# Layer 2 two inner blocks behind layer 1 in a fused attention and MLP kernel, with a third buffer for the inner activations

## The chip, the cores and the metric

The kernel runs on one core of a Trainium2 chip. TensorE (PE) multiplies, VectorE (DVE), ScalarE (ACT) and GpSimd (POOL) work on elements, and SyncE's queue (SP) issues the transfers. Each engine takes its instructions strictly in the order in which the program lists them, and waits at the head of its list for semaphores of the others. The metric is the time of one execution in microseconds (us); smaller is better.

## What is computed

Attention with two kinds of masks gives x, a mixing over the tokens of low rank is added to it, and a two-layer MLP stands behind:

```python
scores = scale * np.matmul(q, k.transpose(0, 1, 3, 2))        # B=8, H=8, S=576, D=64
scores = np.where(masks[None, :, :, :], scores, -1000000000.0)  # a window of 32 keys, plain or dilated by 4
attn = softmax(scores); x = np.matmul(attn, v)                 # x: 8 x 576 x 512
h = xt @ U @ V                                                 # rank 32, over the tokens
u = x + h.transpose(0, 2, 1)
ch = np.maximum(u @ w_ch1, 0.0) @ w_ch2                        # 512 -> 2048 -> 512
return (u + ch).astype(np.float32)
```

## The kernel before, in words

The 4608 tokens are 36 tiles of 128. The MLP takes them in twelve **chunks** of three tiles (384 tokens). The 2048 inner features are sixteen **inner blocks** of 128 (`f` from 0 to 15). All products that must be exact to float32 are split into a high and a low part (names ending in h and l), and three of the four products of parts are taken.

For each chunk the loop at L761 goes over the sixteen inner blocks. `layer1(f)` (L732) issues twelve matmuls (L738) into one PSUM tile `ph`: four with the high weights and high input `uth`, four with the low weights, four with the low input `utl`. ACT then makes the high half of the rectified result, `hh` (L743), and DVE the low half, `hl`, from `ph` and `hh` (L744). `layer2(f)` (L748) issues nine matmuls (L755) from `hh` and `hl` into the chunk's three accumulators `acc`. Before the change the loop issues layer 1 of block f and then layer 2 of block f-1. At the chunk's end DVE adds the accumulators to x (L780), and SP sends the tiles out (L781).

Three sets of buffers close this circle. `ph` has two buffers in PSUM, so `layer1(f+2)` can't start before ACT and DVE have read `ph` of block f. `hh` and `hl` have two each in SBUF (L741, L742). The three accumulators have one buffer each, so the next chunk's first layer 2 waits for L780.

Between the matmuls the loop calls `slot()`, which pops due work from a sorted queue (L726): attention of the next batches (scores `s` L376 and L387, masks and maxima on DVE L404 and L407, exponentials on ACT L411, transposes of the probabilities `pt` on DVE L437 and L440, products `pv` L448, their scaling L476), the mixing over tokens (`xhl` L494 and L496, `t` L516, `ts` L525 to L531, `m` L540, sum L542), and the transposes `xt` of x for the next chunks (L556), sixteen small DVE instructions for each tile. ACT and DVE turn these into `uth` and `utl` (L571, L572). In the first chunk the loop also calls `weight_step` (L262), which narrows the weights from eight-byte numbers on ACT, DVE and POOL (L202 to L220).

The program text doesn't fix the order on an engine. A scheduler goes over the instructions with a timeline of its own, and lists on each engine the ready instruction with the highest priority, which is its place in the program text. So a change to the text also moves work of the attention, on all engines.

## Time and profile before

| what | value |
|---|---|
| median of three runs | 1083.85 us (1081.57 to 1084.34) |
| span of the profiled execution, first to last instruction | 1079.6 us |
| time of the profiled execution outside its span | not listed apart; the lowest of the runs is 2.0 us above the span, the median 4.25 us |
| granted TensorE clock, mean | 0.968 |
| PE busy | 1006.9 us, 93% of the span |
| DVE busy | 793.5 us, 73% |
| ACT busy | 407.4 us, 38% |
| POOL busy | 337.7 us, 31% |
| chain that ended last | PE 62%, DVE 28%, DMA 4%, rest 6% |

A row of the timeline gives the start, the duration, the engine, the source line, the operation with output and input, the number of instructions that it merges, and in brackets how long the engine had been idle and what ended that. A row of the stretches gives, for a stretch of the span, its length, then the busy time and the number of instructions of PE, of its weight loads (PEld), of DVE, ACT and POOL, the granted clock of TensorE, and the share and rate of the DMA engines. The page merges twelve or nine matmuls of one block where nothing stands between them. A matmul's own duration is longer than its distance to the next one, since they are pipelined; the distances are what adds up.

### The profile page before, as it was taken

How to read it: one execution, taken by the hardware profiler on the slowest of the kernel's cores; microseconds unless marked ns; L12 is line 12 of the kernel's file. 1: busy time of each engine (PE TensorE's matmuls, PEld its weight loads, DVE VectorE, ACT ScalarE, POOL GpSimd, SP SyncE). 2: the span in 40 equal slices, each digit the busy share in tenths (PEclk: the TensorE clock that was granted, in tenths of full speed). 3: DMA queues.
4: the chain of work that ended last, by engine and by line, in shares of the span. 5: the costliest groups of instructions: out<-in, count | busy, mean ns of one | idle time of the engine just before them, and what ended most of it. 6: DMA issues, size and time to landing. Idle time of an engine off the chain costs nothing.

```text
span 1079.6 us, 17590 instructions
## 1 busy us (share of the span) xinstructions
PE 1006.9 (93%) x5304; PEld 896.3 (83%) x5304; DVE 793.5 (73%) x2688; ACT 407.4 (38%) x1225; POOL 337.7 (31%) x533
## 2 busy tenths in 40 slices
PE   6688888999999999998999999998999999699998
PEld 6468776988888988987888898897888998599997
DVE  6999998788589778787668878888858876921211
ACT  5566645434234533433323442543324542111110
POOL 1567766243132521242312441433214331000000
PEclk9679999999999999998999999998999999999999
DMA  9556633222222420331202430332302320000000
GB/s 290 165 195 206 208 108 108 72 79 64 65 58 69 122 66 22 102 90 50 79 23 61 114 93 23 103 87 57 92 9 71 101 76 16 30 1 1 30 1 30
DMA packets 75599, 87.33 MB, mean 81 GB/s; under 512 B 10448, under 2 KB 66320, under 8 KB 75504
## 3 DMA queue, kind: packets, MB, share of 16 engines
q1 hardware_dynamic: 75504, 86.20, 26.8%
q8 instruction: 43, 0.70, 0.3%
q14 instruction: 52, 0.43, 0.1%
HBM read 72.00 MB, written 9.44 MB: 75 GB/s over the span
## 4 chain that ended last, share of the span: by engine, by line
PE 62%; DVE 28%; DMA 4%; issue 3%; ACT 1%; POOL 1%; SPq 0%; DVEq 0%; ACTq 0%; POOLq 0%
PE ph L738 28%; PE acc L755 27%; DVE xt L556 9%; PE pv L448 3%; DVE v L211 2%; PE s L376 2%; DVE hl L744 2%; DVE pt L437 2%; DVE pt L440 1%; DVE v L207 1%; PE t L516 1%; DVE p L407 1%; DVE x L476 1%; DVE x L542 1%; DVE xp L476 1%
## 5 line engine op out<-in xcount | busy, mean ns | idle before, releaser
L755 PE MATMUL acc<-w2h,hh 128*128 128x512 f32 x576 | 229.7, 399 | 6.8 <-ACT hh L743 4.5
L352 POOL TENSOR_TENSOR qks<-qkr,qks 128x160 fp32r<-128x160 f32 x192 | 103.8, 540 | 414.5 <-ACT qks L351 259.1
L755 PE MATMUL acc<-w2h,hl 128*128 128x512 f32 x576 | 208.3, 403 | 23.6 <-DVE hl L744 23.4
L755 PE MATMUL acc<-w2l,hh 128*128 128x512 f32 x576 | 228.0, 396 | 0.0
L744 DVE SCALAR_TENSOR_TENSOR hl<-ph,hh 128x384 fp32r<-128x384 f32 x192 | 106.1, 554 | 145.7 <-ACT hh L743 144.5
L411 ACT ACTIVATE p<-p,nmax 128x160 f32<-128x160 f32 (+1 forms) x288 | 116.8, 406 | 202.1 <-DVE nmax L407 200.2
L743 ACT ACTIVATE hh<-ph 128x384 fp32r<-128x384 f32 x192 | 93.2, 485 | 237.5 <-PE ph L738 233.3
L738 PE MATMUL ph<-uth,w1l 128*128 128x384 f32 x768 | 177.6, 343 | 0.0
L738 PE MATMUL ph<-uth,w1h 128*128 128x384 f32 x768 | 176.9, 346 | 0.2 <-ACT uth L571 0.2
L738 PE MATMUL ph<-utl,w1h 128*128 128x384 f32 x768 | 175.8, 341 | 0.1
L738 PEld LDWEIGHTS ph<-uth,w1h 128*128 128x128 f32 x768 | 141.9, 193 | 16.0 <-ACT uth L571 0.6
L556 DVE STREAM_TRANSPOSE xt<-x 32x128 f32<-32x128 f32 x480 | 145.2, 302 | 11.9 <-PE t L516 4.6
L755 PEld LDWEIGHTS acc<-w2h,hl 128*128 128x128 f32 x576 | 107.1, 191 | 51.7 <-DVE hl L744 32.0
L738 PEld LDWEIGHTS ph<-uth,w1l 128*128 128x128 f32 x768 | 138.4, 191 | 0.9
L738 PEld LDWEIGHTS ph<-utl,w1h 128*128 128x128 f32 x768 | 137.0, 189 | 1.5 <-DVE utl L572 0.5
L437 DVE STREAM_TRANSPOSE pt<-p 32x128 f32<-32x128 f32 x384 | 115.7, 301 | 18.6 <-ACT p L411 13.4
L755 PEld LDWEIGHTS acc<-w2h,hh 128*128 128x128 f32 x576 | 108.9, 189 | 23.9 <-ACT hh L743 5.3
L755 PEld LDWEIGHTS acc<-w2l,hh 128*128 128x128 f32 x576 | 108.8, 189 | 15.3
L351 ACT CAST qks<-qkr 128x288 fp32r<-128x288 f32 x192 | 80.9, 428 | 99.2 <-PE s L376 61.2
L355 POOL TENSOR_TENSOR qks<-qkr,qks 64x128 fp32r<-64x128 f32 x192 | 89.6, 467 | 15.1
L448 PE MATMUL pv<-v,pt 96*128 96x128 f32 x576 | 81.5, 286 | 9.5 <-issue 2.9
L448 PEld LDWEIGHTS pv<-v,pt 96*128 96x128 f32 x576 | 77.4, 200 | 14.4 <-issue 6.0
(68 smaller groups left out, 1098.4 us busy)
## 6 DMA issues: line engine op xcount, KB each, us to landing
qkr<-qk SPq DMA_DIRECT2D x192, 144.0 KB, 2.1
raw<-w SPq DMA_DIRECT2D x26, 512.0 KB, 4.4
v<-vv SPq DMA_DIRECT2D x126, 96.0 KB, 2.1
out<-x SPq DMA_DIRECT2D x36, 256.0 KB, 2.3
qkr<-qk SPq DMA_DIRECT2D x22, 224.0 KB, 4.3
qk<-qk SPq DMA_DIRECT2D x7, 448.0 KB, 7.2
raw<-w SPq DMA_DIRECT2D x12, 256.0 KB, 3.2
x<-xp SPq DMA_DIRECT2D x88, 32.0 KB, 1.9
```

Source lines behind the costliest of these rows:

```text
L211: nc.vector.scalar_tensor_tensor(out=o, in0=hi, scalar=-0x80000000, in1=o, op0=ALU.bitwise_and, op1=ALU.bitwise_or)
L351: nc.scalar.copy(out=t[:, 0:QK2], in_=raw)
L352: nc.gpsimd.tensor_tensor(out=t[:, QK2:], in0=raw[:, P:], in1=t[:, P:QK2].bitcast(F32), op=ALU.subtract)
L355: eng.tensor_tensor(out=t[lo, 0:P], in0=raw[lo, 0:P], in1=t[lo, 0:P].bitcast(F32), op=ALU.subtract)
L411: nc.scalar.activation(out=p_sb[:, u, 0:w], in_=p_sb[:, u, 0:w], func=AF.Exp, bias=nmax[:, u:u + 1], scale=-1.0, accum_out=ssum[:, u:u + 1],)
L437: nc.vector.transpose(out=to[:, :, WIN * (r % 2):WIN * (r % 2 + 1)], in_=p_sb[rs, :, QB * s + WIN * k:QB * s + WIN * (k + 1)])
L448: nc.tensor.matmul(pv[:, u, :], lhsT=pt[:, u, :], rhs=v_sb[:, u % 2, :], start=True, stop=True)
L556: nc.vector.transpose(out=tp[ks, :, rs], in_=x4[rs, :, ks])
L738: nc.tensor.matmul(ph, lhsT=w[:, k, :], rhs=u[:, k, :], start=(n == 0), stop=(n == len(seq) - 1))
L743: nc.scalar.activation(out=hh, in_=ph, func=AF.Relu)
L744: nc.vector.scalar_tensor_tensor(out=hl, in0=ph, scalar=0.0, in1=hh.bitcast(F32), op0=ALU.max, op1=ALU.subtract)
L755: nc.tensor.matmul(acc[i], lhsT=h[:, ss], rhs=w, start=(f == 0 and n == 0), stop=(f == FC - 1 and n == 2))
```

## The change

Layer 2 of block f-2, and no longer of f-1, follows layer 1 of block f. `hh` and `hl` get three buffers. At a chunk's end the last two blocks of layer 2 follow the loop. The room for the buffers comes from a scratch area in SBUF for dynamic DMA, which shrinks to 1024 bytes a partition. `ph` keeps its two buffers and `acc` its one each.

```diff
+LAG2 = 2
...
+SCRATCH = 1024
...
-            hh = work.tile([P, CTOK], F32R, tag="hh", name=f"hh{c}_{f}", bufs=2)
-            hl = work.tile([P, CTOK], F32R, tag="hl", name=f"hl{c}_{f}", bufs=2)
+            hh = work.tile([P, CTOK], F32R, tag="hh", name=f"hh{c}_{f}", bufs=LAG2 + 1)
+            hl = work.tile([P, CTOK], F32R, tag="hl", name=f"hl{c}_{f}", bufs=LAG2 + 1)
...
-            if f > 0:
-                layer2(f - 1)
+            if f >= LAG2:
+                layer2(f - LAG2)
                 if f < FC - 1:
                     slot()
...
-        layer2(FC - 1)
+        for f in range(FC - LAG2, FC):
+            layer2(f)
...
-    nc = bacc.Bacc("TRN2", target_bir_lowering=False, num_devices=1)
+    nc = bacc.Bacc("TRN2", target_bir_lowering=False, num_devices=1, dynamic_dma_scratch_size=SCRATCH)
```

The two added constants move the later lines: what is L738 before is L740 after, L744 is L746, L755 is L757, L556 is L558. Names below end in the block (for `ph`, `hh`, `hl`) or the tile (for `acc`) and a running number.

**TensorE, fifth chunk, around inner blocks 10 to 13.** Before, PE comes to the low half of block 10 behind six matmuls of its own block, and to `ph` of block 12 behind that:

```order
L755 MATMUL acc_2_4941<-w2h_762,hh_10_5722 128x512
L755 MATMUL acc_2_4941<-w2l_763,hh_10_5722 128x512
L376 MATMUL s_3_5549<-qks_5513 128x320
L448 MATMUL pv_5593<-v_0_5465,pt_75 128x128 x2
L448 MATMUL pv_5593<-v_1_5483,pt_75 128x128 x2
L755 MATMUL acc_0_4939<-w2h_762,hl_10_5723 128x512
L755 MATMUL acc_1_4940<-w2h_762,hl_10_5723 128x512
L755 MATMUL acc_2_4941<-w2h_762,hl_10_5723 128x512
L738 MATMUL ph_12_5876<-uth_4877,w1h_760 128x384 x4
```

Now the same `s` and `pv` of the attention stand behind six matmuls of block 11, and then comes layer 1 of block 13, ahead of the low half of block 11:

```order
L757 MATMUL acc_2_4933<-w2h_762,hh_11_5770 128x512
L757 MATMUL acc_2_4933<-w2l_763,hh_11_5770 128x512
L378 MATMUL s_3_5551<-qks_5518 128x320
L450 MATMUL pv_5598<-v_0_5468,pt_75 128x128 x2
L450 MATMUL pv_5598<-v_1_5486,pt_75 128x128 x2
L740 MATMUL ph_13_5919<-uth_4843,w1h_1384 128x384 x4
L740 MATMUL ph_13_5919<-uth_4843,w1l_1385 128x384 x4
L740 MATMUL ph_13_5919<-utl_4844,w1h_1384 128x384 x4
L757 MATMUL acc_0_4931<-w2h_762,hl_11_5771 128x512
```

`ph_13` takes the buffer of `ph_11`, so the first of these rows that needs `hl_11` to be done is now the one of `ph_13`, a whole block of layer 1 ahead of the matmul that reads `hl_11`.

**VectorE at the same place.** The transposes `xt` of two tiles are due here. Before, they stand between `hl_9` and `hl_10`; these are the last rows of that stretch:

```order
L556 STREAM_TRANSPOSE xt_5643<-x_3813 32x4x32 x3
L407 ISA p_5497,nmax_5498<-s_1_5511,p_5497 128x160
L407 ISA nmax_5498 128x1
L556 STREAM_TRANSPOSE xt_5643<-x_3813 32x4x32 x6
L404 TENSOR_TENSOR p_5497<-s_2_5535,wide_sb 128x160
L556 STREAM_TRANSPOSE xt_5643<-x_3813 32x4x32
L744 SCALAR_TENSOR_TENSOR hl_10_5723<-ph_10_5686,hh_10_5722 128x384
L556 STREAM_TRANSPOSE xt_5643<-x_3813 32x4x32 x4
L744 SCALAR_TENSOR_TENSOR hl_11_5819<-ph_11_5776,hh_11_5818 128x384
```

Now they stand between `hl_10` and `hl_11`, and `hl_11` behind the last of them:

```order
L558 STREAM_TRANSPOSE xt_5645<-x_3815 32x4x32 x8
L409 ISA p_5502,nmax_5503<-s_1_5516,p_5502 128x160
L409 ISA nmax_5503 128x1
L452 RECIPROCAL ssum_5389<-ssum_5389 128x4
L558 STREAM_TRANSPOSE xt_5645<-x_3815 32x4x32 x2
L406 TENSOR_TENSOR p_5502<-s_2_5535,wide_sb 128x160
L558 STREAM_TRANSPOSE xt_5645<-x_3815 32x4x32 x6
L746 SCALAR_TENSOR_TENSOR hl_11_5771<-ph_11_5731,hh_11_5770 128x384
L746 SCALAR_TENSOR_TENSOR hl_12_5881<-ph_12_5849,hh_12_5880 128x384
```

Counted over the whole stretch, from one `hl` to the next, there are 36 transposes, three L404 and two L407 before, and 40 transposes, four of what was L404 and three of what was L407 now; the other rows are the same. The eighth chunk has 36 and 40 at the same place. In the second chunk the same transposes were spread before, 26 ahead of `hl_9` and 13 ahead of `hl_10`; now 40 stand in one piece ahead of `hl_11`.

**TensorE, end of the first chunk.** Here the mixing of the second batch (`t_1`, then `m_0_1` to `m_4_1`) must be done before the second chunk's first tiles can be turned (`tp`). Before, the last `t_1` stands ahead of eight matmuls of layer 1, and the `m` are strewn into layer 2 of block 15:

```order
L516 MATMUL t_1_1615<-xhl_4_1_1648,us 64x256
L738 MATMUL ph_15_1889<-uth_641,w1l_1404 128x384 x4
L738 MATMUL ph_15_1889<-utl_642,w1h_1403 128x384 x4
L540 MATMUL m_0_1_1675<-ts_1_1667,vs 128x256
L540 MATMUL m_1_1_1687<-ts_1_1667,vs 128x256
L540 MATMUL m_2_1_1698<-ts_1_1667,vs 128x256
L755 MATMUL acc_0_764<-w2h_1405,hh_15_1927 128x512
```

Now layers 1 and 2 of block 15 are over when the last seven `t_1` come, and `m` and `tp` follow with no matmul of the MLP between them:

```order
L757 MATMUL acc_2_766<-w2h_1386,hl_15_1894 128x512
L518 MATMUL t_1_1617<-xhl_1_1_1620,us 64x256
L518 MATMUL t_1_1617<-xhl_2_1_1629,us 64x256 x2
L518 MATMUL t_1_1617<-xhl_3_1_1642,us 64x256 x2
L518 MATMUL t_1_1617<-xhl_4_1_1653,us 64x256 x2
L542 MATMUL m_0_1_1683<-ts_1_1670,vs 128x256
L542 MATMUL m_1_1_1692<-ts_1_1670,vs 128x256
L542 MATMUL m_2_1_1698<-ts_1_1670,vs 128x256
L542 MATMUL m_3_1_1710<-ts_1_1670,vs 128x256
L542 MATMUL m_4_1_1721<-ts_1_1670,vs 128x256
L571 MATMUL tp_1899<-id_sb,x_305 128x128 x4
```

So eight matmuls of layer 1 and nine of layer 2 that lay between the last `t_1` and the first `tp` now lie ahead of it.

**VectorE at that place.** Before, the last `xhl`, which the last `t_1` need, comes straight ahead of `ts_1`, and the three sums of the accumulators only later:

```order
L496 TENSOR_TENSOR xhl_4_1_1648<-x_1039,xhl_4_1_1648 128x256
L526 TENSOR_TENSOR ts_1_1667<-t_1_1615,ts_1_1667 32x256
L542 TENSOR_TENSOR x_344<-x_344,m_0_1_1675 64x256
L744 SCALAR_TENSOR_TENSOR hl_15_1928<-ph_15_1889,hh_15_1927 128x384
L542 TENSOR_TENSOR x_890<-x_890,m_1_1_1687 128x256
```

Now all three stand ahead of `ts_1`, and two of them ahead of the last `xhl`:

```order
L783 TENSOR_TENSOR x_178<-acc_0_764,x_178 128x512
L783 TENSOR_TENSOR x_219<-acc_1_765,x_219 128x512
L498 TENSOR_TENSOR xhl_4_1_1653<-x_1087,xhl_4_1_1653 128x256
L783 TENSOR_TENSOR x_261<-acc_2_766,x_261 128x512
L528 TENSOR_TENSOR ts_1_1670<-t_1_1617,ts_1_1670 32x256
L544 TENSOR_TENSOR x_344<-x_344,m_0_1_1683 64x256
```

`hl_15`, which stood behind the first sum of `m`, now stands ahead of all of these.

## The prediction

> **What bounds the kernel now.** I read the page first: PE is busy for 93% of the span, and no other engine comes near.
>
> ```profile
> span 1079.6 us, 17590 instructions
> PE 1006.9 (93%) x5304; PEld 896.3 (83%) x5304; DVE 793.5 (73%) x2688; ACT 407.4 (38%) x1225; POOL 337.7 (31%) x533
> ```
>
> The 72.7 us in which PE is idle are not spread evenly, so next I took the stretches (length, then PE, PEld, DVE, ACT, POOL busy, clock, DMA):
>
> ```profile
> 40.00:80.00 40.00, 29.90 (x123) 23.94 (x123) 37.97 (x83) 21.94 (x56) 26.70 (x22) 0.63 0.49 162
> 80.00:120.00 40.00, 34.86 (x199) 31.73 (x199) 39.15 (x93) 25.23 (x64) 31.11 (x24) 0.96 0.64 203
> 120.00:160.00 40.00, 33.64 (x193) 28.93 (x193) 38.42 (x128) 21.19 (x70) 25.94 (x25) 1.00 0.45 140
> ...
> 200.00:920.00 720.00, 699.86 (x3748) 627.92 (x3747) 565.63 (x2033) 274.20 (x844) 220.68 (x414) 0.99 0.24 69
> 920.00:948.00 28.00, 19.45 (x81) 15.94 (x80) 26.80 (x80) 3.26 (x7) 0.00 (x0) 0.85 0.08 29
> ```
>
> From 40 to 160 us, the start and most of the first chunk, DVE is busy for 115.5 of 120 us: it sets the pace there, and a longer lead of PE gives nothing but DVE's own 4.5 idle us. From 200 to 920 us PE is idle for 720 - 699.9 = 20.1 us only, and from 920 to 948 us for 8.6 us, again under a full DVE. These 28.7 us are all that a better order can win behind the first chunk, besides what a lowered clock costs. The waits of PE say what they are:
>
> ```profile
> PE acc L755 <- DVE hl L744: 23.4, 20, 2.5
> ...
> PE acc L755 <- ACT hh L743: 4.5, 3, 3.3
> ...
> 105.01 0.50 PE L755 MATMUL acc<-w2h,hh 128*128 128x512 f32 x1 [3.28 <-ACT hh L743]
> ```
>
> (The last row is from the timeline.) Twenty waits of layer 2 for the low half, 23.4 us, none over 2.5 us. This is what the change aims at. The timeline shows where the longest sit. In the fifth chunk:
>
> ```profile
> 474.04 1.05 PE L448 MATMUL pv<-v,pt 96*128 96x128 f32 x8
> ...
> 474.80 0.56 DVE L744 SCALAR_TENSOR_TENSOR hl<-ph,hh 128x384 fp32r<-128x384 f32 x1 [0.83 <-ACT hh L743]
> ...
> 479.26 2.19 DVE L556 STREAM_TRANSPOSE xt<-x 32x128 f32<-32x128 f32 x7
> ...
> 481.48 0.33 DVE L404 TENSOR_TENSOR p<-s,wide_sb 128x160 f32<-128x160 f32 x1
> ...
> 485.90 0.33 DVE L407 CUSTOM_DVE_ANT_0 p<-s,p 128x160 f32<-128x160 f32 x1
> ...
> 486.38 0.38 PE L376 MATMUL s<-qks 128*128 128x320 f32 x1 [2.51 <-DVE nmax L407]
> ...
> 487.66 1.13 PE L448 MATMUL pv<-v,pt 96*128 96x128 f32 x8 [0.90 <-DVE nmax L407]
> ...
> 490.20 0.56 DVE L744 SCALAR_TENSOR_TENSOR hl<-ph,hh 128x384 fp32r<-128x384 f32 x1
> ...
> 490.81 1.65 PE L755 MATMUL acc<-w2h,hl 128*128 128x512 f32 x3 [2.02 <-DVE hl L744]
> ```
>
> DVE does `hl` of block 9 at 474.80 and that of block 10 at 490.20. The 15.4 us between are full of transposes for the next chunk. PE runs out of work and waits three times, 2.51 + 0.90 + 2.02 = 5.4 us. The same burst returns at 735 us. The one in the second chunk is milder, with one wait of 2.09 us:
>
> ```profile
> 735.00:739.00 4.00, 1.51 (x6) 0.75 (x5) 3.80 (x14) 0.90 (x3) 0.00 (x0) 0.91 0.23 69
> 739.00:742.00 3.00, 2.31 (x9) 2.05 (x10) 2.80 (x11) 0.84 (x3) 0.97 (x2) 0.50 0.09 22
> ...
> 237.70 0.98 PE L755 MATMUL acc<-w2h,hl 128*128 128x512 f32 x3 [2.09 <-DVE hl L744]
> ```
>
> **The rate of a block.** The chain of work shows both blocks where nothing disturbs them, and layer 1 behind the wait at 490:
>
> ```profile
> 247.00 2.07 PE acc L755 x9
> ...
> 260.64 2.12 PE ph L738 x12
> ...
> 492.45 3.72 PE ph L738 x12
> ```
>
> A block of layer 2 is 2.07 us (0.23 a matmul), one of layer 1 2.12 us (0.177).
>
> **Term 1, what the lead is worth.** The groups of the two steps that read `ph`, and the one queue that holds all transfers of data:
>
> ```profile
> q1 hardware_dynamic: 75504, 86.20, 26.8%
> ...
> L744 DVE SCALAR_TENSOR_TENSOR hl<-ph,hh 128x384 fp32r<-128x384 f32 x192 | 106.1, 554 | 145.7 <-ACT hh L743 144.5
> ...
> L743 ACT ACTIVATE hh<-ph 128x384 fp32r<-128x384 f32 x192 | 93.2, 485 | 237.5 <-PE ph L738 233.3
> ```
>
> No instruction is added or taken away: the same 5304 matmuls, the same 192 `hh` and `hl`, the same DMAs. The moved step issues matmuls alone; the sums L780 and the sends L781 still follow the chunk's last layer 2. Before, `hl` of block f is needed one block of layer 2, one of layer 1 and two to six matmuls of its own block after `ph` of f is done: 2.07 + 2.12 + 0.46 to 1.38 = 4.65 to 5.57 us of PE's work. One would think that the change adds a block of each kind, 4.2 us. It doesn't: `ph` still has two buffers, and layer 1 of f+2 now comes ahead of layer 2 of f and can't start before DVE has read `ph` of f, which is done by this very L744. So the need is at 2.07 + 2.12 + 2.07 = 6.26 us, and the gain per wait is 0.7 to 1.6 us. The wait only changes its name, from `acc` for `hl` to `ph` for `hl`. Of the 20.1 us behind 200 us, 5.4 are the fifth chunk's burst and (4 - 1.51) + (3 - 2.31) = 3.2 the eighth's, 2.1 the second's: 9.4 are left for small waits. Two things hold the gain on these back: where it is the last block of a chunk, layer 2 follows layer 1 as closely as before, and where a wait is under 0.7 us only that is won. The bounds are -9.4 (all vanish) and 0 (the scheduler's new order makes as many). I take -4.5.
>
> **Term 2, the bursts.** The scheduler gives DVE's transposes the room that the later need leaves: the burst of the fifth chunk has four transposes, one L404 and one L407 more. By the rows above (2.19 / 7 = 0.31 each, 0.33, 0.33) it grows by 1.25 + 0.66 = 1.9 us to 17.3 us. PE's work between the end of `ph` of the block ahead of it and the matmul that waits, counted on the two orders: before, 24 matmuls of layer 2, 24 of layer 1, 5 `s` and 8 `pv`; now 33, 24, 5 and 8. That is nine more of layer 2, 2.07 us. So the wait changes by 1.9 - 2.07 = -0.2 us. The same for the eighth chunk (36 to 40 transposes) and, with less certainty, for the end of the attention at 940 us. Together -0.6. In the second chunk the burst was split in 26 and 13 transposes, and is now one of 40: it should cost what the fifth chunk's costs, 5.2 us, where 2.1 stood: +3.1. The bounds are +3.1 and, if the burst still comes in two parts, the -1.6 of term 1.
>
> The clock adds to this. Stretches around the fifth chunk's burst and the second's:
>
> ```profile
> 235.00:239.00 4.00, 1.91 (x9) 1.33 (x8) 3.76 (x13) 0.30 (x1) 0.00 (x0) 1.00 0.14 37
> ...
> 484.00:488.00 4.00, 0.72 (x4) 0.55 (x5) 3.77 (x15) 1.30 (x5) 0.00 (x0) 1.00 0.08 24
> 488.00:491.00 3.00, 0.98 (x9) 0.79 (x8) 2.82 (x9) 0.44 (x3) 0.98 (x2) 0.68 0.33 85
> 491.00:495.00 4.00, 4.00 (x12) 3.71 (x13) 3.44 (x14) 0.89 (x4) 0.00 (x0) 0.50 0.09 30
> ```
>
> Behind the 5.4 us of waits the granted clock is 0.50, and the block of layer 1 takes 3.72 us in place of 2.12: 1.6 us more. Behind 2.1 us it stays at 1.00. A wait of 5.2 us in the second chunk would cost 1.6 us there too, one of 3 us perhaps not: +0.8 taken, between 0 and 1.6. The Trainium skill says it as a rule ("TensorE: Matmul & The Clock Gate", Part 1: The HAM clock gate): an idle window of about 3.4 us puts TensorE to half its clock until a busy window has passed. The trace agrees, with 0.50; by the rule the full 1.6 us would be due, and the sum 0.8 us higher.
>
> **Term 3, the end of the first chunk.** What of the mixing was covered by layer 1 and 2 of block 15 now isn't. Rows of before:
>
> ```profile
> 169.90 1.51 DVE L219 CAST w2h<-v 128x512 fp32r<-128x512 f32 x1
> ...
> 176.26 0.86 PE L755 MATMUL acc<-w2h,hl 128*128 128x512 f32 x3
> ...
> 176.79 1.88 DVE L780 TENSOR_TENSOR x<-acc,x 128x512 f32<-128x512 f32 x3
> ...
> 179.06 1.42 PE L569 MATMUL tp<-id_sb,x 128*128 128x128 f32 x8 [1.53 <-DVE x L542]
> ...
> 183.65 1.52 PE L738 MATMUL ph<-uth,w1h 128*128 128x384 f32 x4
> ```
>
> Uncovered are 8 x 0.177 + 9 x 0.23 = 3.5 us of PE's work, and up to 1.88 us of the sums L780 now stand ahead of `ts_1`. Against that, layers 1 and 2 of block 15 are done sooner: DVE is the pace here, and up to the last cast of weights its list is shorter than before by the work of the mixing that moved behind it (in place of the cast at 169.90, several us earlier). In one order the chain stands beside the weights, in the other behind them, and DVE's total is the same. The bounds are -4.5 us (all of DVE's idle time of the first chunk) and +5.4 us. I take -2, nearer to the row that shows DVE full.
>
> **The third buffer and the scratch.** They issue nothing, and all loads and stores of the program stand in the one queue q1 above, so I see no user of the scratch that would wait. I cost it at nothing; if some transfer did slow down, it would have the 73% of that queue's time in which nothing moves as cover.
>
> **Sum.** -4.5 - 0.6 + 3.1 + 0.8 - 2 = -3.2; with the waits of PE for `hh` of ACT (4.5 us in three; the longest, 3.3 us, stands at 105 us in the first chunk, where DVE sets the pace), which lie a block further away now, -1.2 more: -4.4 us. It is worked out on the span of 1079.6 us. The median of the runs, 1083.85 us, stands 4.25 us above, and the difference is carried over: **1079.5 us**. A measurement of this kernel can tell about 0.3%, 3.3 us, from no change.
>
> **The rivals.**
> *The lead works in full.* If the reading of `ph` doesn't come to bind, each wait shrinks by a block of layer 2 beyond term 1: the 9.4 us of small waits go, and the three late bursts lose 2.07 us each; with term 3 that is -9.4 - 6.2 - 2 = -17.6, 1066 us. For it speaks that ACT and DVE may have read `ph` long before; against it the two buffers, and DVE's place in the list. The Trainium skill ("Perfetto Trace Analysis", Identifying Performance Opportunities) holds that a gap which keeps returning on the engine that should be full can mean too few buffers for the next tile. By it one would expect this rival; no row here tells whether the lacking buffer is `hh`/`hl` or `ph`.
>
> *Slower, by the uncovered mixing.* Term 3 comes out at +5.4: the second chunk starts at 183.65 + 5.4. The rest of the sum stays at -2.4, or at -0.9 with the small waits at -3: 1083.85 + 4.5 = 1088.4 us. It decides at the last cast of weights: if that doesn't start at least 3.5 us sooner than at 169.90, the uncovered part is lost. For it speaks the order; against it DVE's 115.5 of 120 us.
>
> *No change.* Small waits win as little as the second chunk loses, and term 3 is zero: 1083.9 us, 1081 to 1087. For it speaks that DVE's total stays the same, and that PE has only 20 us to win.
>
> **How the numbers follow.** My forecast, waits that move to `ph` with a small gain, has 0.50, and its own range is 1076.5 to 1083 us, so that 0.31 lie below 1080.6 us and 0.19 within 0.3%. The lead in full has 0.15, the uncovered mixing 0.22, no change 0.13. Faster: 0.31 + 0.15 = 0.46. Within 0.3%: 0.19 + 0.13 = 0.32. Slower: 0.22. The range goes from 1070 us, which leaves out most of the lead in full, to 1090 us, which leaves out the uppermost of the uncovered mixing, 0.2 together.
>
> **What would show it.** In the new profile the wait "acc for hl" should fall from 23.4 us to below 8, and a new one, `ph` for `hl`, should stand at 10 to 18 us, with its longest pieces in the second, fifth and eighth chunk ahead of layer 1 of block 13, and a clock of 0.50 behind them. PE's idle time from 200 to 920 us should stay between 14 and 20 us. The last cast of weights should come 3 us or more ahead of 169.90, and the first `ph` of the second chunk near 181.7. The forecast is wrong if no wait of `ph` for `hl` appears, or if the second chunk starts behind 185.

## The result, and the profile after

The changed kernel takes 1088.70 us (median of ten runs, 1086.80 to 1093.76), the kernel before 1083.96 us beside it: a ratio of 1.0053, 95% interval 1.0037 to 1.0069. It is slower by 4.7 us, where the forecast was 4.4 us faster. The time lies inside the forecast's range, but in the case that had 0.22, the uncovered mixing.

The profiled execution of the changed kernel took 1093.76 us, 5 us over its median. Of these, 3.8 us come ahead of the first layer 1, which starts at 68.40 in place of 64.63, though DVE, ACT and POOL have run the same number of instructions up to there. In the profiles of e1 to e6, which have the same text up to there, this start lies between 64.97 and 67.86, so it is taken as chance. Times below that start at a chunk's first `hh` leave it out.

The page of the changed kernel, its first lines:

```profile
span 1092.0 us, 17583 instructions
PE 1016.8 (93%) x5304; PEld 907.2 (83%) x5304; DVE 794.1 (73%) x2688; ACT 408.5 (37%) x1225; POOL 336.0 (31%) x533
```

The waits of PE, changed kernel (engine, what waits, who releases: us, times, longest):

```profile
PE ph L740 <- DVE hl L746: 17.9, 8, 4.8
...
PE acc L757 <- DVE hl L746: 4.8, 4, 1.7
...
PE acc L757 <- ACT hh L745: 1.6, 3, 0.9
```

The wait has changed its name as forecast: "acc for hl" is down from 23.4 to 4.8, and a new one, `ph` for `hl`, stands at 17.9. The two together, 22.7 us, are hardly less than the 23.4 before.

Where the time went is seen when the run is cut at the chunks' first `hh`: first chunk, second chunk, third to last. The kernel before, then the changed one (length, then PE, PEld, DVE, ACT, POOL busy, clock, DMA):

```profile
69.72:188.11 118.39, 100.30 (x538) 86.14 (x537) 111.33 (x310) 67.48 (x197) 83.46 (x80) 0.96 0.53 167
188.11:271.16 83.05, 80.34 (x440) 72.35 (x439) 70.21 (x267) 35.56 (x114) 29.78 (x57) 1.00 0.26 74
271.16:1075.61 804.45, 777.69 (x4084) 697.26 (x4082) 554.33 (x1923) 265.14 (x792) 196.85 (x369) 0.99 0.20 57
```

```profile
73.68:199.42 125.74, 107.70 (x530) 92.85 (x529) 107.90 (x294) 66.61 (x189) 80.90 (x75) 0.88 0.49 155
199.42:287.44 88.02, 84.27 (x445) 76.21 (x444) 73.24 (x274) 36.10 (x115) 30.98 (x59) 0.96 0.27 75
287.44:1088.01 800.57, 773.60 (x4081) 695.33 (x4080) 555.13 (x1932) 266.49 (x800) 196.50 (x373) 0.99 0.20 57
```

The first chunk is 7.4 us longer, the second 5.0, and the ten others together 3.9 shorter. So the loss sits at the front. The ten others aren't shorter by less waiting: PE is idle there for 26.8 us before and 27.0 now, and busy for 4.1 us less. In the second chunk DVE has 3.0 us more work than before, in the first 3.4 us less: work of the attention has slipped from one into the other.

The end of the first chunk, from the timelines of the engines of the changed kernel, in order of time:

```profile
167.73 1.29 POOL L222 TENSOR_TENSOR w2l<-v,w2h 128x512 fp32r<-128x512 f32 x1
...
169.05 0.75 ACT L204 ACTIVATE v<-raw 128x256 f32<-128x256 f32 x2 [0.62 <-POOL w2l L222]
...
169.90 0.43 DVE L209 TENSOR_SCALAR v<-v 128x512 int32<-128x512 int32 x1 [5.09 <-ACT v L204]
...
174.23 1.05 PE L450 MATMUL pv<-v,pt 96*128 96x128 f32 x8
...
175.19 1.49 DVE L221 CAST w2h<-v 128x512 fp32r<-128x512 f32 x1 [1.33 <-POOL v L215]
...
177.51 1.21 DVE L478 TENSOR_TENSOR spare<-pv,ssum 64x128 f32<-64x128 f32 x4
...
178.12 3.56 SPq L482 DMA_DIRECT2D x<-spare  x5
...
179.84 0.40 ACT L496 CAST xhl<-x 64x256 fp32r<-64x256 f32 x1 [5.36 <-DMA x<-spare]
...
182.84 0.86 PE L757 MATMUL acc<-w2h,hl 128*128 128x512 f32 x3
...
187.26 2.13 PE L542 MATMUL m<-ts,vs 128*128 128x256 f32 x5 [1.72 <-ACT ts L533]
189.19 1.92 PE L571 MATMUL tp<-id_sb,x 128*128 128x128 f32 x8
...
193.77 1.65 PE L740 MATMUL ph<-uth,w1h 128*128 128x384 f32 x4 [0.30 <-ACT uth L573]
```

The same steps before:

```profile
156.50 1.05 PE L448 MATMUL pv<-v,pt 96*128 96x128 f32 x8
...
161.41 3.04 SPq L480 DMA_DIRECT2D x<-spare  x5
...
164.33 0.40 ACT L494 CAST xhl<-x 64x256 fp32r<-64x256 f32 x1
```

Two things are to be seen. First, a serial chain across the engines: the last PV of batch 1, its scaling, the transfer into x, the split `xhl`, the mixing `t`, `ts`, `m`, and only then the transposes `tp` and layer 1 of the second chunk. Counted from the chunk's first layer 1, its PV came at 156.50 - 64.63 = 91.9 us before and comes at 105.8 us now. Before, the chain ran beside the last weights; now it runs behind them, and from the last matmuls of layer 2 (182.84) to the next layer 1 (193.77), 10.9 us, PE has only the chain's own small steps and a few scores. Before, from 176.26 to 183.65, that took 7.4 us. And the last matmuls of layer 2 come later too: 114.4 us behind the chunk's first layer 1, in place of 111.6. Together the second chunk's layer 1 comes 6.4 us later: 2.8 for layer 2, 3.5 for the longer stretch behind it.

Second, DVE stands idle for 5.09 us at the head of its list and waits for weights, behind ACT, which in turn waited 0.62 us for POOL's L222. DVE is not the pace there now. The last cast of weights, 169.90 before, comes at 175.19, or 171.4 without the later start: not sooner, but 1.5 us later.

The clock adds to it. Stretches behind the chain's waits, of the changed kernel and then of the kernel before:

```profile
184.00:188.00 4.00, 1.50 (x8) 1.00 (x6) 2.29 (x6) 1.08 (x3) 0.00 (x0) 0.91 0.67 234
188.00:192.00 4.00, 3.63 (x15) 2.81 (x14) 2.90 (x8) 1.45 (x3) 0.00 (x0) 0.50 0.00 0
192.00:196.00 4.00, 3.70 (x13) 3.12 (x12) 2.36 (x10) 2.67 (x10) 2.56 (x6) 0.50 0.14 37
```

```profile
180.00:184.00 4.00, 3.21 (x13) 2.31 (x13) 3.05 (x10) 3.85 (x14) 1.79 (x5) 0.73 0.37 115
184.00:188.00 4.00, 4.00 (x21) 4.00 (x21) 3.55 (x16) 1.55 (x6) 2.29 (x5) 0.84 0.42 113
```

Now there are at least eight us at half the clock; before, the clock fell here too, but for a shorter time (a mean of 0.73 and 0.84 over eight us). The first four matmuls of layer 1 take 1.65 us now and took 1.52 before, where four such take 0.87 at full clock (at 163.68 us). Over the whole first chunk PE is idle for 18.0 us now and 18.1 before, and busy for 7.4 us longer at a mean clock of 0.88 in place of 0.96. But e2 below, with the same front, has a clock of 0.94, 22.1 us of idle time and a first chunk nearly as long, 123.5 us: the end of the chunk is what counts, not how PE spends the time up to it.

Of the four longest waits of `ph` three stand where they were forecast, in the second, fifth and eighth chunk; the fourth, 3.36 us, stands at 956.41, in the eleventh:

```profile
260.07 1.65 PE L740 MATMUL ph<-uth,w1h 128*128 128x384 f32 x4 [2.97 <-DVE hl L746]
...
510.75 1.65 PE L740 MATMUL ph<-uth,w1h 128*128 128x384 f32 x4 [2.33 <-DVE hl L746]
...
760.57 1.54 PE L740 MATMUL ph<-uth,w1h 128*128 128x384 f32 x4 [4.78 <-DVE hl L746]
```

### The profile page after: what moved, and what is told of

Read it like the earlier page. It is cut to its first block, busy times and chain, and to the rows that moved or that the text cites. A ratio compares the mean times of both kernels' runs of the same rounds, so it can differ in the third digit from the quotient of the medians.

```text
span 1092.0 us, 17583 instructions
## 1 busy us (share of the span) xinstructions
PE 1016.8 (93%) x5304; PEld 907.2 (83%) x5304; DVE 794.1 (73%) x2688; ACT 408.5 (37%) x1225; POOL 336.0 (31%) x533
## 4 chain that ended last, share of the span: by engine, by line
PE 66%; DVE 21%; DMA 5%; issue 3%; ACT 2%; POOL 1%; SPq 0%; DVEq 0%; POOLq 0%; ACTq 0%
PE ph L740 30%; PE acc L757 27%; DVE xt L558 7%; PE pv L450 4%; PE s L378 2%; DVE v L213 2%; DVE pt L439 2%; PE t L518 1%; DVE v L209 1%; DVE hl L746 1%; DMA qkr<-qk 1%; DVE utl L574 1%; PE m L542 1%; DVE xp L478 1%; DVE x L478 1%
## 5 line engine op out<-in xcount | busy, mean ns | idle before, releaser
L354 POOL TENSOR_TENSOR qks<-qkr,qks 128x160 fp32r<-128x160 f32 x192 | 102.7, 535 | 426.2 <-ACT qks L353 208.2
L757 PE MATMUL acc<-w2h,hh 128*128 128x512 f32 x576 | 229.0, 398 | 1.8 <-ACT hh L745 1.6
L757 PE MATMUL acc<-w2l,hh 128*128 128x512 f32 x576 | 227.2, 394 | 0.0
L757 PE MATMUL acc<-w2h,hl 128*128 128x512 f32 x576 | 216.0, 397 | 4.8 <-DVE hl L746 4.8
L746 DVE SCALAR_TENSOR_TENSOR hl<-ph,hh 128x384 fp32r<-128x384 f32 x192 | 105.5, 554 | 150.8 <-ACT hh L745 149.5
L740 PE MATMUL ph<-uth,w1h 128*128 128x384 f32 x768 | 181.4, 349 | 18.8 <-DVE hl L746 17.9
L740 PE MATMUL ph<-utl,w1h 128*128 128x384 f32 x768 | 177.3, 345 | 2.1 <-DVE utl L574 2.1
L740 PE MATMUL ph<-uth,w1l 128*128 128x384 f32 x768 | 178.6, 346 | 0.0
L740 PEld LDWEIGHTS ph<-uth,w1h 128*128 128x128 f32 x768 | 140.1, 193 | 35.7 <-DVE hl L746 22.0
L558 DVE STREAM_TRANSPOSE xt<-x 32x128 f32<-32x128 f32 x480 | 145.1, 302 | 11.2 <-PE t L518 4.0
L740 PEld LDWEIGHTS ph<-utl,w1h 128*128 128x128 f32 x768 | 139.3, 192 | 3.1 <-DVE utl L574 2.8
L740 PEld LDWEIGHTS ph<-uth,w1l 128*128 128x128 f32 x768 | 139.9, 193 | 0.2
L757 PEld LDWEIGHTS acc<-w2h,hl 128*128 128x128 f32 x576 | 108.5, 190 | 26.0 <-DVE hl L746 6.5
L757 PEld LDWEIGHTS acc<-w2h,hh 128*128 128x128 f32 x576 | 108.8, 189 | 22.4 <-ACT hh L745 3.4
L757 PEld LDWEIGHTS acc<-w2l,hh 128*128 128x128 f32 x576 | 108.7, 189 | 16.6
L450 PE MATMUL pv<-v,pt 96*128 96x128 f32 x576 | 83.7, 290 | 12.8 <-issue 5.5
```

What stands on the lines that cost most here:

```text
L354: nc.gpsimd.tensor_tensor(out=t[:, QK2:], in0=raw[:, P:], in1=t[:, P:QK2].bitcast(F32), op=ALU.subtract)
L450: nc.tensor.matmul(pv[:, u, :], lhsT=pt[:, u, :], rhs=v_sb[:, u % 2, :], start=True, stop=True)
L558: nc.vector.transpose(out=tp[ks, :, rs], in_=x4[rs, :, ks])
L740: nc.tensor.matmul(ph, lhsT=w[:, k, :], rhs=u[:, k, :], start=(n == 0), stop=(n == len(seq) - 1))
L746: nc.vector.scalar_tensor_tensor(out=hl, in0=ph, scalar=0.0, in1=hh.bitcast(F32), op0=ALU.max, op1=ALU.subtract)
L757: nc.tensor.matmul(acc[i], lhsT=h[:, ss], rhs=w, start=(f == 0 and n == 0), stop=(f == FC - 1 and n == 2))
```

## The experiments

The theory at the outset: the loss is made at the end of the first chunk, where the mixing lost its cover. One rival puts it into the bursts of the later chunks, another into the third buffer and the scratch. What lies behind the loss of cover is a count. `slot()` gives out the work of the attention by its own count (`pos = c + slots / 93`), and layer 2 holds three of these calls for each block. With a lead of two, three fewer calls stand ahead of the same block of layer 1: whatever the queue gives out comes half an inner block later against layer 1. So the change is two changes, the lead and this shift. Where the count of slots is begun at 3 the shift is taken back, and at -3 it is made without the lead. At a chunk's end this isn't exact: by the program the last call there stands at 90 of 93 before, at 89 in the change, at 92 with the lead and a start at 3, and at 87 without the lead and a start at -3. What is due behind it falls into the next chunk.

All ratios are to the kernel before on the same chip, with 95% intervals. Lines are those of the experiment's own file, a line or so off the changed kernel's.

**e1, the lead of two from the second chunk on only.**

```diff
         slots = [0]
+        lag = 1 if c == 0 else LAG2
...
-            if f >= LAG2:
-                layer2(f - LAG2)
+            if f >= lag:
+                layer2(f - lag)
...
-        for f in range(FC - LAG2, FC):
+        for f in range(FC - lag, FC):
```

> The first chunk goes back to a lead of one block, the other eleven keep two; buffers and scratch as in the changed kernel. Theory (the loss sits at the end of the first chunk, where the batch's mixing has lost its cover): 1083 to 1085 us, the second chunk's layer 1 starts about 119 us after the first one's, as before. Rival 1 (the loss comes from the later chunks, whose bursts of VectorE stand in one piece): 1087 to 1090 us. Rival 2 (the third buffer and the smaller scratch, which move other tiles, cost it): 1087 to 1090 us.

Measured: 1074.58 us, ratio 0.990 (0.9884 to 0.9916). In the later chunks the change wins about 10 us, far more than any theory here gave it. The windows of e1, first chunk, second chunk, the rest:

```profile
73.14:191.96 118.82, 101.70 (x532) 86.84 (x531) 111.30 (x310) 67.73 (x197) 83.36 (x80) 0.94 0.53 168
191.96:275.32 83.36, 80.91 (x440) 72.08 (x439) 70.33 (x268) 34.46 (x113) 29.33 (x57) 1.00 0.26 73
275.32:1070.28 794.96, 774.73 (x4084) 697.11 (x4082) 554.01 (x1924) 263.00 (x792) 194.25 (x369) 0.99 0.20 58
```

Front as before, the rest 9.5 us shorter. The waits of PE from the second chunk on, before and in e1:

```profile
PE acc L755 <- DVE hl L744: 18.8, 15, 2.5
PE s L376 <- DVE nmax L407: 3.6, 2, 2.5
PE pv L448 <- DVE nmax L407: 2.7, 2, 1.8
PE acc L755 <- DVE x L780: 2.2, 1, 2.2
```

```profile
PE ph L741 <- DVE hl L747: 11.2, 5, 3.4
PE pv L450 <- issue: 2.8, 2, 2.2
PE acc L758 <- DVE hl L747: 2.7, 2, 1.5
...
PE s L378 <- DVE nmax L409: 1.5, 1, 1.5
```

Waiting for `hl` falls from 18.8 to 11.2 + 2.7 = 13.9 us only. The attention's own waits for `nmax`, 6.3 us, fall to 1.5, and the wait for L780 goes; some new small waits take a part of this back. From the third chunk on PE is idle for 20.2 us in place of 26.8, and busy for 774.7 in place of 777.7.

**e2, the lead of two in the first chunk only** (`lag = LAG2 if c == 0 else 1`).

> The reverse: a lead of two blocks in the first chunk alone, one block in the others. Theory (end of the first chunk): 1088 to 1090 us, layer 1 of the second chunk starts about 125 us after that of the first. Rival 1 (later chunks): 1083 to 1085 us. Rival 2 (buffers and scratch): 1087 to 1090 us, with the start of the second chunk as before.

Measured: 1097.37 us, ratio 1.0114 (1.01 to 1.0129), 13 us slower than before, more than expected. First chunk 123.5 us, second 87.8, the rest 806.5. Its front is close to the change's, without the later start of that profile. The two halves, -9.9 us in e1 and +12.9 here, sum to +3.0, near the change's +4.7.

**e3, buffers and scratch alone** (`lag = 1` in all chunks).

> Three buffers and the smaller scratch, but a lead of one block in every chunk. Theory and rival 1: 1083 to 1085 us, no change against before. Rival 2 (buffers and scratch): 1087 to 1090 us.

Measured: 1083.73 us, ratio 0.9997 (0.9986 to 1.0007). In this order the third buffer and the smaller scratch cost and give nothing; that rival falls.

**e4, the changed kernel with the shift taken back** (`slots = [3]`).

> The changed kernel with its count of slots in every chunk begun at 3 in place of 0. The longer lead takes three calls of slot() away ahead of each block of layer 1, so that the queued attention and mixing come half a block later; this puts them back to the same block of layer 1. Theory (the mixing lost its cover because its slots moved): 1082 to 1085 us, the second chunk starts about 119 us after the first. Rival 1 (bursts of the later chunks): 1087 to 1090 us. Rival 2 (buffers and scratch): 1087 to 1090 us.

Measured: 1080.56 us, ratio 0.9959 (0.9947 to 0.9971), 10 us under the change by the ratios. First chunk 124.1 us, second 84.4, the rest 793.4. The shift carries the loss; but the second chunk doesn't start where the theory had it, and the lead in the first chunk still leaves that chunk 5.7 us longer than before.

**e9, the shift without the lead, in the first chunk only** (`lag = 1`, `slots = [0 if c else -3]`).

> The order before, lead of one block in all chunks; only in the first chunk the count of slots is begun at -3, so that the attention and the mixing stand half an inner block later against layer 1, as in the changed kernel, without its lead. Theory M (what the change loses in the first chunk is the cover of the mixing, which the shift of the slots takes away): most of the 13 us of e2 is here too, 1092 to 1098 us. Theory W (it is the lead itself, which leaves more of layer 2 behind the last weights): 1081 to 1087 us.

Measured: 1106.81 us, ratio 1.0212 (1.019 to 1.0234). Not 13 but 23 us slower. The first chunk, and its last PV:

```profile
72.80:199.72 126.92, 106.63 (x534) 92.31 (x533) 108.07 (x294) 65.94 (x189) 80.19 (x75) 0.89 0.48 154
```

```profile
175.31 1.05 PE L450 MATMUL pv<-v,pt 96*128 96x128 f32 x8
```

The chunk is as long as in the change, and the PV as late, without any lead. Theory W, the lead itself, falls as the main cause, and M (the cover) is confirmed in kind and too small in size: the later chunks lose as well here (second 89.7, the rest 815.3), for which M has no reason.

**e13, batch 1's pieces alone put back** in the changed kernel:

```diff
-        queue += [(lo + (hi - MARGIN - lo) * at_, it) for at_, it in its]
+        early_by = 3 / (6 * FC - 3) if b == 1 else 0.0
+        queue += [(lo + (hi - MARGIN - lo) * at_ - early_by, it) for at_, it in its]
```

> The changed kernel, lead of two blocks everywhere, slots as the change has them; only the due positions of batch 1's pieces (its attention and its mixing) are set 3 slots earlier, so that these stand in the first chunk where they stood against layer 1 before. Theory M (the loss is the cover that batch 1's pieces lose at the end of the first chunk): it goes as in e4, 1077 to 1082 us. Rival O (the loss hangs on the other pieces that stand later too: loads, the split of the scores to come, the turning of x): 1086 to 1091 us.

Measured: 1086.60 us, ratio 1.0033 (1.002 to 1.0047). By its time that is rival O's number. The windows split it:

```profile
70.75:190.13 119.38, 102.75 (x534) 89.30 (x533) 109.71 (x291) 66.10 (x185) 79.72 (x71) 0.91 0.52 161
190.13:278.98 88.85, 84.42 (x445) 76.01 (x444) 73.25 (x278) 36.77 (x121) 31.78 (x63) 0.96 0.26 74
```

The first chunk is back at 119.4 us: its loss hung on batch 1's pieces, and M holds for it. The second stays at 88.9 us with 73.25 us of DVE, as in the change; something else slips into it. The whole is hardly faster than the change (1.0053).

**e15, all slots of the first chunk put back** in the changed kernel (`slots = [0 if c else 3]`), and **e16, batch 2's pieces as well as batch 1's** (as e13, with `b < 3`).

> The changed kernel, lead of two blocks everywhere, with the count of slots begun at 3 in the first chunk alone. Theory F (the whole loss comes from the shift of the slots in the first chunk; the second chunk is long since pieces that were due at the end of the first one fall into it): first chunk 119 to 124 us, second chunk 82 to 85 us, 1077 to 1082 us in all. Rival G (the second chunk is long by its own slots under the lead of two): second chunk 87 to 89 us, 1084 to 1088 us.

> e13 with batch 2's pieces set 3 slots earlier as well; they are due from 0.9 of the first chunk on, through the second and third. If batch 2's pieces are what falls from the end of the first chunk into the second: second chunk 82 to 85 us, 1077 to 1083 us. If other pieces are (loads ahead, the turning of x): second chunk 87 to 89 us, 1084 to 1088 us.

Measured: e15 1078.70 us, ratio 0.9963 (0.9948 to 0.9977); e16 1084.46 us, 1.0015 (1.0002 to 1.0027). The windows of e15, first and second chunk:

```profile
72.07:196.03 123.96, 105.81 (x536) 91.77 (x536) 113.81 (x310) 69.39 (x197) 84.16 (x80) 0.89 0.52 161
196.03:279.42 83.39, 80.94 (x440) 71.96 (x439) 70.43 (x267) 34.51 (x113) 29.31 (x57) 1.00 0.26 73
```

Theory F holds: putting back the slots of one chunk takes 10 us off the change. By the windows more than half of it comes off later, though: the first chunk is 1.8 us shorter than in the change, the second 4.6, and the ten others, whose slots are the change's, 5.6 (795.0 us). In e16 the second chunk falls to 83.8 us too, so batch 2's pieces, due from 0.9 of the first chunk on, are what slipped; but the first chunk is 125.4 us there, and the whole misses the time expected. The ten others are at 796.0 us, against 800.7 in e13, so the loss there goes with batch 2's pieces too, which e16 also moves in the second and third chunk; how isn't shown. With the lead in the first chunk, that one is long where batch 2's first pieces run inside it, and where they don't the second is: the two together are 201.4 us before, 213.8 in the change, 211.4 in e2, 208.2 in e13, 207.4 in e15, 209.2 in e16. With a lead of one in the first chunk and its slots as before, both are short.

The end of the first chunk, counted in us from its first layer 1:

| run | last matmuls of layer 2 | second chunk's layer 1 | between them |
|---|---|---|---|
| before | 111.6 | 119.0 | 7.4 |
| changed | 114.4 | 125.4 | 10.9 |
| e2 | 114.4 | 124.8 | 10.4 |
| e13 | 116.4 | 120.2 | 3.8 |
| e15 | 116.1 | 123.7 | 7.6 |

Putting the pieces back gives the chain its cover again (3.8 us between in e13, 7.6 in e15). What it doesn't bring back is the end of layer 2, which is later still.

**Is it the lead that wins in the later chunks?** e1 has the lead and the shift there. **e5** is e1 with the shift taken back (`slots = [3 if c else 0]`); **e6** has the shift without the lead (`lag = 1`, `slots = [-3 if c else 0]`).

> As e1 (lead of one block in the first chunk, of two from the second on), with the count of slots begun at 3 instead of 0 from the second chunk on, so that the attention stands again where it stood against layer 1 before the change. Theory L (the gain of e1 is the lead: one more block of matmuls stands ahead of the wait for hl): the gain stays, 1072 to 1077 us. Theory S (the gain of e1 comes from the attention, which is taken up half an inner block later against layer 1): the gain goes, 1081 to 1085 us.

> The order before (lead of one block in all chunks, three buffers held but two in use at a time), with the count of slots begun at -3 from the second chunk on, so that the attention stands against layer 1 as in the changed kernel. Theory L: no lead, no gain, 1082 to 1087 us. Theory S: the gain of e1 without its lead, 1074 to 1077 us.

Measured: e5 1074.56 us, ratio 0.9922 (0.9905 to 0.9939); e6 1070.99 us, 0.9888 (0.987 to 0.9907). Each theory is right where it forecasts a gain and wrong where it forecasts none: the lead alone wins 8 us, the shift alone 12, both together 10. e6 even lies below the range that its theory gave. The wait of PE for `hl` in e6 from the second chunk on:

```profile
PE acc L758 <- DVE hl L747: 9.6, 10, 2.0
```

It is halved without any lead, and lower than in e1. The attention's pieces stand otherwise against `hl` there; which of them matter isn't shown.

**How much hangs on the place?** Three more places from the second chunk on: **e10** (`lag = 1`, slots from -6), **e11** (`lag = 1`, slots from 3), **e12** (lead of two, slots from -3, so a whole block later than before). In all three the first chunk is as before.

> Lead of one block, the count of slots begun at -6 from the second chunk on: the attention stands a whole inner block later against layer 1. Theory B (e6 gained because its bursts happen to fall better against hl; the gain is one of place, not of being late): somewhere between 1070 and 1086 us, no further gain on e6. Theory D (the later the attention, the better): 1062 to 1069 us.

> Lead of one block, the count of slots begun at 3 from the second chunk on: the attention stands half an inner block earlier against layer 1 than in the kernel before. Theory B: between 1074 and 1090 us. Theory D: 1088 to 1096 us.

> e1 (lead of one block in the first chunk, of two later) with the count of slots begun at -3 from the second chunk on: the attention stands a whole inner block later against layer 1 than before, as in e10, but with the lead of two. Theory B (the lead takes up the same waits that a better place takes away, and makes the time depend less on the place): 1070 to 1077 us whatever the place. Theory D: 1060 to 1068 us.

| attention against layer 1 | lead of one | lead of two |
|---|---|---|
| half a block earlier | e11 1.0057 (1.0038 to 1.0076) | not run |
| as before | 1 | e5 0.9922 (0.9905 to 0.9939) |
| half a block later | e6 0.9888 (0.987 to 0.9907) | e1 0.990 (0.9884 to 0.9916) |
| a whole block later | e10 0.9959 (0.9943 to 0.9974) | e12 0.9876 (0.9857 to 0.9896) |

(1090.76 us for e11, 1079.24 for e10, 1070.74 for e12.) The waits for `hl` from the second chunk on, e10, e11 and e12:

```profile
PE acc L758 <- DVE hl L747: 19.2, 16, 2.8
```

```profile
PE acc L758 <- DVE hl L747: 17.8, 14, 2.7
```

```profile
PE ph L741 <- DVE hl L747: 11.2, 4, 3.4
PE acc L758 <- DVE hl L747: 2.2, 2, 1.1
```

Theory D falls by e10 and e12: later is not always better. (e11 alone lies in D's range and 0.8 us above B's.) What B says of the place holds: with a lead of one, the place alone moves the time over 18 us (1.0057 to 0.9888). Over the three places that both leads have, it is 12 us with a lead of one and 5 with two. At the best place the lead wins nothing; at the two others with a partner it wins 8 and 9 us. What it buys is that the time hangs less on where the attention stands. The waits for `hl` don't explain these times by themselves: against the 18.8 us before, e10 has 19.2 and is faster, e11 17.8 and is slower. PE's whole idle time from the third chunk on does go with them here, with 26.8 us before, 25.0 in e10 and 30.7 in e11, and so does its busy time, with 777.7, 775.0 and 780.7. e12 and e6 are the best kernels of the study, 13.0 and 11.7 us under the one before.

**e7 and e8, three buffers for `ph`**, at a lead of one and as e1; the bank is taken from the tiles of the attention and the mixing (`bufs=3` to `2` for the pool, `bufs=2` to `3` for `ph`).

> The order before, with PSUM dealt out anew: three buffers for ph, two instead of three for the scores, PV, t, m and the transposes. It is the base for e8. With a lead of one block layer 1 hardly ever waits for a ph buffer, so the third one gives nothing in either theory; the missing buffer of the others costs something: 1085 to 1105 us.

> e1 (lead of two blocks from the second chunk on) with the PSUM of e7, three buffers for ph. Theory P (the two ph buffers hold back part of the lead: e1 still waits 11.2 us at layer 1 for hl to free one): those waits go, and the kernel is 14 to 22 us faster than e7. Theory N (what waits there is late for the same DVE work with a third ph, and the wait only moves back to layer 2): 8 to 11 us faster than e7, as e1 is against the kernel before.

Measured: 1264.08 us (1.1673, 1.1651 to 1.1695) and 1265.22 us (1.1691, 1.1666 to 1.1716). Both miss what was expected by far, and they settle nothing. With two banks the scores wait for their readers (48.1 us in 11 waits of `s` for `nmax`, the largest of e8 behind 190 us), and the lead is worth nothing there. Whether the two buffers of `ph` hold the lead back stays open.

**e14, e12 with the first chunk's slots begun at 3**, half a block earlier than before.

> e12 (lead of one block in the first chunk, of two later with slots from -3) with the slots of the first chunk begun at 3: batch 1's pieces stand half a block earlier against layer 1 than in the kernel before. Theory M: at the old place the last pieces of the mixing still stand behind the last layer 2, so that more cover may gain a little, but the weights set the end there: 1066 to 1072 us. Rival E (the attention that comes earlier stands ahead of the weights on VectorE and delays them): 1074 to 1082 us.

Measured: 1076.40 us, ratio 0.9938 (0.9921 to 0.9954), and a first chunk of 123.3 us in place of e12's 119.3. Rival E's number: standing earlier wins nothing, and the last cast of weights comes 111.0 us behind the first layer 1, where it came 105.3 behind it before. Of the three places tried with a lead of one (e9, before, e14) the one before is the best for the first chunk.

## Why the prediction was right or wrong

**The step that failed is term 3.** It read: "layers 1 and 2 of block 15 are done sooner: DVE is the pace here", and took -2 us with bounds of -4.5 and +5.4. They are done later: the last matmuls of layer 2 come 2.8 us later in the chunk, in the changed kernel and in e2 alike. With the longer stretch behind them the second chunk's layer 1 comes 6.4 us later in the changed kernel's profile and 5.8 in e2's, above the upper bound. That turns the sign of the whole sum.

The reason given for "sooner" doesn't hold in the new order. DVE's 115.5 of 120 us were read up to 160 us and carried on to 176. In the kernel before, DVE is still busy for 9.29 us of the ten from 160 to 170. In the same ten us of the changed kernel's chunk, from 163.77 to 173.77, it is busy for 4.84, and 5.09 us there go on one wait for weights that ACT and POOL still have in hand. A shorter list on DVE does nothing for work that isn't waiting for that list. The last cast of weights comes 1.5 us later; the rest of the 2.8 isn't taken apart.

The uncovered part was priced at 3.5 us, by the matmuls that no longer lay in that stretch, and the stretch is 3.5 us longer (3.0 in e2). The size is right, but the agreement is partly luck. The last PV of batch 1 comes 14.0 us later in the chunk, which the prediction hadn't read, and the chain behind it has a transfer in it and steps of PE at half the clock.

And the cause, that `slot()` counts calls of layer 2, wasn't named: the lead moves everything in the queue. That is why pieces of batch 2 slipped into the second chunk as well. e1 and e15, where they don't slip, are 5.6 us shorter than the change in the ten later chunks as well.

**The rival "slower, by the uncovered mixing"** named the place, the sign and the test (the last cast of weights: it came later, not 3.5 us sooner), and its 1088.4 us is within 0.3 us of the measured time. That is partly luck. It priced the end of the first chunk at +5.4 and all behind it at -0.9, where the profiles, the changed one being 5 us over its median, have +7.4 and +1.1; and e1 shows that what lies behind could be near -9.

**Terms 1 and 2, the later chunks.** Forecast were -4.5, -0.6, +3.1, +0.8 and -1.2, together -2.4 us. The changed kernel has +5.0 in the second chunk and -3.9 in the others. Term 1's gain isn't in its waits: from the second chunk on PE waits for `hl` for 17.6 + 4.8 = 22.4 us, against 18.8 before. In e1, where the first chunk is left alone, that gain is about as small as term 1 said, 18.8 to 13.9 us. The rest of e1's -9.9 lies in waits that aren't for `hl` and that a burst spreads to `s` and `pv` (6.3 to 1.5 us), in the one for L780 (2.2 to 0), and in PE's shorter busy time. Nor is the gain the lead's alone, as term 1 has it: e6 has it all without a lead. The wait for `hh` did fall, from 4.5 to 1.6 us.

The second chunk's burst had +3.1 for its wait and +0.8 for the clock, +3.9 in all, near the +5.0 measured, but by other parts. The wait is 2.97 us in place of the 5.2 expected, 0.9 over the one before. The clock fell all the same, and the block of layer 1 behind it took

```profile
260.07 4.21 PE ph L740 x12
```

2.1 us over 2.12. In e1 this burst stands in three pieces (17, 14 and 9 transposes, from one `hl` to the next), and the second chunk is at 83.4 us against 83.1. The mean clock of the second chunk is 0.96 in all four runs where batch 2's pieces slip (the change, e2, e9, e13) and 1.00 in e1, e4, e15 and e16.

**The third buffer and the scratch** cost nothing with a lead of one, as forecast (e3).

**The signs.** "acc for hl" below 8: 4.8. `ph` for `hl` at 10 to 18: 17.9, with three of its four longest pieces in the chunks named, and a clock of 0.50 behind them. PE idle from 200 to 920 us between 14 and 20: it was 23.0, outside. The last cast and the second chunk's start: both missed, and the second chunk started behind 185, one of the two points at which the forecast was to be called wrong.

**The rule on returning gaps.** The Trainium skill ("Perfetto Trace Analysis", Identifying Performance Opportunities) says that the same gap, repeated on the engine that should be full, can mean too few buffers for the next tile. Here the third buffer alone gives 0.9997 (e3), and e6, with the same buffers and the same lead as e3, halves the waits by its order alone. So the waits that return here can be halved without another buffer. Whether a third `ph` would have done it too isn't shown, since e7 and e8 settle nothing.

What stays open: why the shift alone costs 23 us (e9) where the lead with the same shift costs 13 (e2). By the windows most of the difference lies from the third chunk on, +10.8 us in e9 and +2.1 in e2. The last call of `slot()` in e9's first chunk stands two counts sooner than in e2's, so that more is left for the second chunk; that this is the reason isn't tried. Open too is the 5 us that the lead leaves in the first chunk with the slots put back (124.0 us in e15, 118.8 in e1). e13 and e16 differ in batch 2's pieces alone, and have 119.4 and 125.4 us there, so it hangs on these; in e4 and e15 the last PV comes in time (92.3 and 92.2 us behind the first layer 1), but the last cast of weights only at 111.6.

## What to carry to other kernels

Before a step is moved, ask what counts on it: a queue that is paced by calls inside the step is moved with it, and a small shift can put the head of a serial chain behind the work that used to hide it. Don't carry the reading that one engine sets the pace past the stretch in which it was read: with another order another engine can set it. And where one reordering wins, try the same shift without the idea and the idea without the shift, since a place in the order alone can be worth more than the idea.

## What the runs showed of the hardware

The granted clock stayed at 0.50 from 188 to 196 us, while PE was busy for 3.63 and 3.70 of 4 us, and rose only in the next stretch (0.81). The Trainium skill ("TensorE: Matmul & The Clock Gate", Part 1: The HAM clock gate) gives about 3.4 us of sustained work for the way back to full clock. The trace took longer, with gaps of 0.2 to 0.3 us in that work; what "sustained" allows isn't shown by a run here. It took longer without a gap as well: behind the wait that ends at 260.07 us PE has no idle time, and the clock is at 0.50 up to 265 us.

```profile
260.00:265.00 5.00, 4.93 (x15) 4.75 (x16) 4.80 (x20) 1.42 (x5) 0.00 (x0) 0.50 0.18 44
265.00:266.00 1.00, 1.00 (x5) 0.91 (x4) 0.83 (x4) 0.09 (x1) 0.00 (x0) 0.61 0.01 3
```

The single wait of 2.97 us ahead of this, behind eight small matmuls of PV, was followed by half the clock, where one of 2.09 us before left it at 1.00. In the eighth chunk the clock fell only when a wait of 4.78 us was over: 1.00 from 756 to 760 us, with PE idle throughout, and 0.59 from 760 to 764.
